# A causal convolution and a three-way maxout layer: one product moved out of the maximum, another order of the stages, a band built by a skewed DMA

## The chip, the cores and the metric

The kernel runs on one core of a Trainium2 chip. The metric is device time in microseconds (us), the median over several executions. All executions reported here are fast ones: granted clock of TensorE (the share of its full clock that the profile records) between 0.987 and 1.0 over the whole span, and times of one kernel within about 0.5% of each other. In the profile, PE is TensorE, PEld its weight loads, DVE VectorE, ACT ScalarE, POOL GpSimd, SP SyncE; a trailing q (SPq, ACTq) is the queue of that engine, from which DMAs are issued. L238 is a line of the kernel's source; line numbers differ between the kernels. PSUM is the memory into which TensorE's products are written in these kernels; ACT and DVE copy or combine them from there. The chain is the work that ended last, followed back step by step to what released it.

## The reference, cut to what matters

```
# x: 8 x 4160 x 192 fp32; weight: 8 heads x 7 taps; w1, w2, w3: 192 x 768; w_out: 768 x 192
w = softmax(weight)                                   # 7 taps for each head of 24 channels
y[s] = sum_k w[head, k] * x[s - 6 + k]                # zeros ahead of each batch's first row
h = maximum(maximum(y @ w1, y @ w2), y @ w3)          # 33280 tokens x 768
out = h @ w_out                                       # 33280 x 192, fp32
```

The 33280 tokens are handled as 65 blocks of 512: 64 whole ones, and one made of the last 64 rows of each of the 8 batches (the "ragged" block).

## The kernel before

For each block, TensorE does the convolution as 40 small matmuls against a banded matrix of the taps (two PSUM tiles G1, G2, 32 rows per head), and ACT copies the result to fp16 (xctA, xctB). The first layer runs per slice of 128 hidden columns, six slices in all: three products of two 512-column matmuls each, one ACT copy and two DVE maxima. The second layer (`emit_st2`) runs for the block before, as 4 x 6 matmuls of 192 columns, all of them between the convolution and the first layer.

```
def emit_st2(t, out_sb):
    for s in range(ceil(N / P)):
        pso = psu.tile([P, NBLK], FP32, tag="ps")
        for j in range(NJ):                                   # NJ = 6
            nc.tensor.matmul(pso[0:ms, 0:D], lhsT=hT[:, j, P * s : P * s + ms], rhs=wo[:, j, :],
                             start=(j == 0), stop=(j == NJ - 1))
        nc.scalar.copy(out=out_sb[0:ms, s, :], in_=pso[0:ms, 0:D])

for t in range(NB):                                           # NB = 65
    emit_xdma(t + 3)
    emit_conv(t, G1, G2)
    if prev is not None:
        emit_st2(tp, out_sb_p)                                # second layer of the block before
    nc.scalar.copy(out=xctA[:, 0:N], in_=G1[:, 0:N])
    nc.scalar.copy(out=xctB[:, 0:N], in_=G2[:, 0:N])
    # ... store of the block before ...
    for j in range(NJ):
        for i in range(3):                                    # w1, w2, w3
            nc.tensor.matmul(psw[i][:, 0:N], lhsT=wg[i][0][:, jj], rhs=xctA[:, 0:N], start=True, stop=False)
            nc.tensor.matmul(psw[i][:, 0:N], lhsT=wg[i][1][:, jj], rhs=xctB[:, 0:N], start=False, stop=True)
        nc.scalar.copy(out=t1[:, 0:N], in_=psw[0][:, 0:N])
        nc.vector.tensor_max(out=t12[:, 0:N], in0=t1[:, 0:N], in1=psw[1][:, 0:N])
        nc.vector.tensor_max(out=hT_t[t][:, j, 0:N], in0=t12[:, 0:N], in1=psw[2][:, 0:N])
        if j == 0:
            emit_xcast(t + 3)                                 # x to fp16, on ACT
```

At the start, DVE builds the band of the convolution from masks and taps (56 instructions), and ACT casts the weights.

The softmax here doesn't subtract the row's maximum and nothing guards it: scores larger than these inputs give would overflow.

Of the kernel before, what the change touches and what calls it, by code (L numbers as in the profile page):

```python
# [7 lines left out]

FP32 = mybir.dt.float32  # L10
FP16 = mybir.dt.float16
INT32 = mybir.dt.int32
AXX = mybir.AxisListType.X
ALU = mybir.AluOpType
# [9 lines left out]
NBLK = 512  # L24


@with_exitstack
def kernel(
# [9 lines left out]
):  # L38
    nc = tc.nc

# [5 lines left out]

    blocks = []
# [4 lines left out]
    segs = []  # L52
    off = 0
    for b in range(B):
        s = nfull * NBLK
        while s < SEQ:
            n = min(SEQ - s, NBLK - off)
            segs.append((b, s, n, off))
            off += n
            s += n  # L60
            if off == NBLK:
                blocks.append(segs)
                segs = []
                off = 0
# [5 lines left out]
    def conv_chunks(blk):  # L70
        res = []
        q = 0
        for (b, S, N, off) in blk:
            qq = 0
            while CHK * qq < N:
                o_lo = CHK * qq
                o_hi = min(o_lo + CHK, N)
                row_lo = max(0, S + o_lo - PAD)
                rlen = min(P, SEQ - row_lo)
                cc_lo = o_lo - (row_lo - S)  # L80
                res.append((q, b, row_lo, rlen, off + o_lo, off + o_hi, cc_lo))
                q += 1
                qq += 1
        return res

    NQMAX = max(len(conv_chunks(blk)) for blk in blocks)

    const = ctx.enter_context(tc.tile_pool(name="const", bufs=1))
    wpool = ctx.enter_context(tc.tile_pool(name="wpool", bufs=1))
    xfp = ctx.enter_context(tc.tile_pool(name="xfp", bufs=4))  # L90
    x16p = ctx.enter_context(tc.tile_pool(name="x16p", bufs=4))
    xctp = ctx.enter_context(tc.tile_pool(name="xctp", bufs=2))
    tmpp = ctx.enter_context(tc.tile_pool(name="tmpp", bufs=2))
    htp = ctx.enter_context(tc.tile_pool(name="htp", bufs=2))
    outp = ctx.enter_context(tc.tile_pool(name="outp", bufs=2))

    psg = ctx.enter_context(tc.tile_pool(name="psg", bufs=2, space=bass.MemoryType.PSUM))
    psu = ctx.enter_context(tc.tile_pool(name="psu", bufs=6, space=bass.MemoryType.PSUM))

    wraw = const.tile([P, NHEAD, KW], FP32)  # L100
    nc.sync.dma_start(
        out=wraw[:],
        in_=bass.AP(tensor=weight.tensor, offset=0, ap=[[0, P], [KW, NHEAD], [1, KW]]),
    )
    idx = const.tile([P, BAND_W], INT32)
    nc.gpsimd.iota(out=idx[:], pattern=[[1, BAND_W]], base=0, channel_multiplier=-1)

    x16_t = {}

    def emit_xdma(t):  # L110
        if not (0 <= t < NB):
            return
        chunks = conv_chunks(blocks[t])
        xf32 = xfp.tile([P, NQMAX, D], FP32, tag="xf32", name=f"xf32_{t}")
        x16 = x16p.tile([P, NQMAX, D], FP16, tag="x16", name=f"x16_{t}")
        x16_t[t] = (xf32, x16, [])
        i = 0
        n = len(chunks)
        while i < n:
            jx = i  # L120
            while (
                jx + 1 < n
                and chunks[jx][3] == P
                and chunks[jx + 1][3] == P
                and chunks[jx + 1][1] == chunks[jx][1]
                and chunks[jx + 1][2] - chunks[jx][2] == CHK
            ):
                jx += 1
            (q0, b0, row_lo0, rlen0, _, _, _) = chunks[i]
            cnt = jx - i + 1  # L130
            if cnt > 1:
                src = bass.AP(
                    tensor=x.tensor,
                    offset=(b0 * SEQ + row_lo0) * D,
                    ap=[[D, P], [CHK * D, cnt], [1, D]],
                )
                nc.sync.dma_start(out=xf32[:, i : jx + 1, :], in_=src)
                x16_t[t][2].append((slice(0, P), slice(i, jx + 1)))
            else:
                nc.sync.dma_start(  # L140
                    out=xf32[0:rlen0, q0, :], in_=x[b0, row_lo0 : row_lo0 + rlen0, :]
                )
                x16_t[t][2].append((slice(0, rlen0), slice(q0, q0 + 1)))
            i = jx + 1

    def emit_xcast(t):
        if not (0 <= t < NB):
            return
        (xf32, x16, parts) = x16_t[t]
        for (ps, qs) in parts:  # L150
            nc.scalar.copy(out=x16[ps, qs, :], in_=xf32[ps, qs, :])  # L151

    for u in range(min(3, NB)):
        emit_xdma(u)
        emit_xcast(u)

    wexp = const.tile([P, NHEAD, KW], FP32)
    nc.scalar.activation(out=wexp[:], in_=wraw[:], func=AF.Exp)  # L158
    wsum = const.tile([P, NHEAD], FP32)
    nc.vector.reduce_sum(out=wsum[:], in_=wexp[:], axis=AXX)  # L160
    wrec = const.tile([P, NHEAD], FP32)
    nc.vector.reciprocal(out=wrec[:], in_=wsum[:])
    wnrm = const.tile([P, NHEAD, KW], FP32)
    for h in range(NHEAD):
        nc.vector.tensor_scalar_mul(
            out=wnrm[:, h, :], in0=wexp[:, h, :], scalar1=wrec[:, h : h + 1]
        )
    masks = const.tile([P, KW, BAND_W], FP32)
    for a in range(KW):
        nc.vector.tensor_scalar(  # L170
            out=masks[:, a, :],
            in0=idx[:],
            scalar1=float(a),
            scalar2=None,
            op0=ALU.is_equal,
        )
    bacc = [
        const.tile([P, BAND_W], FP32, tag=f"bacc{h}", name=f"bacc{h}")
        for h in range(NHEAD)
    ]  # L180
    band = const.tile([P, NHEAD, BAND_W], FP16)
    for k in range(KW):
        a = KW - 1 - k
        for h in range(NHEAD):
            if k == 0:
                nc.vector.tensor_scalar_mul(  # L186
                    out=bacc[h][:], in0=masks[:, a, :], scalar1=wnrm[:, h, 0:1]
                )
            else:
                nc.vector.scalar_tensor_tensor(  # L190
                    out=bacc[h][:],
                    in0=masks[:, a, :],
                    scalar=wnrm[:, h, k : k + 1],
                    in1=bacc[h][:],
                    op0=ALU.mult,
                    op1=ALU.add,
                )
            if k == KW - 1:
                nc.scalar.copy(out=band[:, h, :], in_=bacc[h][:])  # L199

    def slot_ranges(half):
        if half == 0:
            return [(32 * g, GRP * g, GRP) for g in range(4)]
        return [(32 * g, 96 + GRP * g, GRP) for g in range(3)] + [(104, 168, GRP)]

    wg = []
    for i, wsrc in enumerate((moe_w1, moe_w2, moe_w3)):
        halves = []
        for half in range(2):
            stage = wpool.tile([P, DFF], FP32, tag=f"wstage{i}{half}")  # L210
            nc.vector.memset(stage[:], 0.0)  # L211
            for (s0, c0, cnt) in slot_ranges(half):
                nc.sync.dma_start(  # L213
                    out=stage[s0 : s0 + cnt, :], in_=wsrc[c0 : c0 + cnt, :]
                )
            wt = wpool.tile([P, DFF], FP16, tag=f"w{i}{half}")
            nc.scalar.copy(out=wt[:], in_=stage[:])  # L217
            halves.append(wt)
        wg.append(halves)

    wo_stage = wpool.tile([P, NJ, D], FP32)
    nc.sync.dma_start(out=wo_stage[:], in_=moe_w_out.rearrange("(j p) c -> p j c", p=P))
    wo = wpool.tile([P, NJ, D], FP16)
    nc.scalar.copy(out=wo[:], in_=wo_stage[:])

    out_2d = out

    hT_t = {}

    def emit_conv(t, G1, G2):  # L230
        (_, x16, _) = x16_t[t]
        for (q, b, row_lo, rlen, out_lo, out_hi, cc_lo) in conv_chunks(blocks[t]):
            ncols = out_hi - out_lo
            for h in range(NHEAD):
                g = h % 4
                gt = G1 if h < 4 else G2
                cb = GRP * h if h < NHEAD - 1 else GRP * h - 8
                nc.tensor.matmul(  # L238
                    gt[32 * g : 32 * g + 32, out_lo:out_hi],
                    lhsT=x16[0:rlen, q, cb : cb + 32],  # L240
                    rhs=band[0:rlen, h, cc_lo : cc_lo + ncols],
                    start=True,
                    stop=True,
                    tile_position=(0, 32 * g),
                )

    def emit_st2(t, out_sb):
        N = blkN[t]
        hT = hT_t[t]
        for s in range(ceil(N / P)):  # L250
            ms = min(P, N - P * s)
            pso = psu.tile([P, NBLK], FP32, tag="ps", name=f"pso_{t}_{s}")
            for j in range(NJ):
                nc.tensor.matmul(  # L254
                    pso[0:ms, 0:D],
                    lhsT=hT[:, j, P * s : P * s + ms],
                    rhs=wo[:, j, :],
                    start=(j == 0),
                    stop=(j == NJ - 1),
                )  # L260
# [20 lines left out]
    for t in range(NB):  # L281
# [17 lines left out]
        for j in range(NJ):  # L299
# [27 lines left out]
            if j == 0:  # L327
                emit_xcast(t + 3)
# [38 lines left out]
```

## Time and profile before

| kernel before | value | where from |
|---|---|---|
| median time | 772.04 us (771.39 to 773.94, four runs) | times |
| profiled span, granted clock | 770.3 us, 0.997 | profile |
| busy: TensorE, DVE, ACT | 90%, 68%, 56% | page, engine totals |
| one block of 512 tokens | 11.31 us (mean over 60 blocks) | timeline |
| 512-column, 192-column matmul, start to start | 0.216, 0.083 us | timeline |
| stall ahead of the seventh second-layer matmul | 0.78 us, or 0.35 more in some blocks | timeline |

To read it: the page's busy share of TensorE counts matmuls that overlap, so it does not say how much of a block is work. Only the distances in the timeline do. The shares of the chain by line show whose time counts towards the end:

```profile
PE psw L306 27%; PE psw L313 27%; PE pso L254 14%; DVE t L323 11%; DVE hT L324 7%; PE G L238 1%; DVE bacc L190 1%; DMA wo_stage<-in_moe_w_out_dram 1%; DVE stage L211 1%; ACT wt L217 0%; DVEq L324 0%; ACT t L322 0%; DVE bacc L186 0%; SPq L213 0%; ACT outsb L261 0%
```

The three products are 54% of it (L306, L313), the second layer 14%, and the two maxima on DVE (L323, L324) another 18%: the last maximum of a block is what the second layer then waits for.

### The profile page before, as it was taken

To read this page: it belongs to the slowest core of one execution; us is meant where nothing else is said; L and a number is where in the kernel's file an instruction comes from. 1 tells how busy PE (TensorE), PEld (TensorE's weight loads), DVE (VectorE), ACT (ScalarE), POOL (GpSimd) and SP (SyncE) were. 2 spreads that over 40 slices of the span, in tenths; PEclk is the share of its full clock that TensorE was granted. 3 is DMA by queue.
4 is the path that set the end of the run, shared out by engine and by line. 5 is a ranking of instruction groups with operands and counts; after the bars stand their busy time and mean duration, and the time that the engine had idled before them with its cause. 6 is when DMAs were issued, how large, how long until landed. Compare 5 with 4: busy or idle time off the path is not lost.

```text
span 770.3 us, 16387 instructions
## 1 busy us (share of the span) xinstructions
PE 696.2 (90%) x6524; PEld 386.6 (50%) x6524; DVE 527.1 (68%) x859; ACT 429.1 (56%) x885; POOL 0.4 (0%) x5
## 2 busy tenths in 40 slices
PE   0799999999999999999999999999999999999996
PEld 0355555555545554555555555555455545555543
DVE  9476766676676677667667666766766766676674
ACT  3666555556555555555555555555555555556552
POOL 0000000000000000000000000000000000000000
PEclk9999999999999999999999999999999999999998
DMA  6342223133133223313322322331332233111101
GB/s 183 121 143 54 86 91 89 52 93 93 52 88 93 68 73 91 93 49 93 93 52 88 94 76 63 94 93 50 91 92 60 81 93 88 48 43 42 34 31 42
DMA packets 78829, 60.69 MB, mean 79 GB/s; under 512 B 2880, under 2 KB 78176, under 8 KB 78752
## 3 DMA queue, kind: packets, MB, share of 16 engines
q1 hardware_dynamic: 78752, 59.64, 26.3%
q8 instruction: 51, 0.84, 0.5%
q14 instruction: 26, 0.21, 0.1%
HBM read 34.07 MB, written 25.56 MB: 77 GB/s over the span
## 4 chain that ended last, share of the span: by engine, by line
PE 68%; DVE 19%; issue 9%; ACT 1%; DMA 1%; DVEq 0%; SPq 0%; ACTq 0%
PE psw L306 27%; PE psw L313 27%; PE pso L254 14%; DVE t L323 11%; DVE hT L324 7%; PE G L238 1%; DVE bacc L190 1%; DMA wo_stage<-in_moe_w_out_dram 1%; DVE stage L211 1%; ACT wt L217 0%; DVEq L324 0%; ACT t L322 0%; DVE bacc L186 0%; SPq L213 0%; ACT outsb L261 0%
## 5 line engine op out<-in xcount | busy, mean ns | idle before, releaser
L306 PE MATMUL psw<-xctA,wt 128*128 128x512 f16 x1170 | 443.8, 380 | 0.8 <-ACT xctA L292 0.3
L313 PE MATMUL psw<-xctB,wt 128*128 128x512 f16 x1170 | 443.7, 380 | 0.5 <-ACT wt L217 0.4
L323 DVE TENSOR_TENSOR t<-t,psw 128x512 f32<-128x512 f32 x390 | 265.2, 681 | 187.3 <-ACT t L322 180.5
L322 ACT COPY t<-psw 128x512 f32<-128x512 f32 x390 | 228.5, 586 | 230.5 <-PE psw L313 220.8
L324 DVE TENSOR_TENSOR hT<-t,psw 128x512 f16<-128x512 f32 x390 | 267.3, 687 | 46.2 <-PE psw L313 8.3
L254 PE MATMUL pso<-wo,hT 128*128 128x192 f16 x1560 | 151.8, 247 | 42.8 <-DVE hT L324 42.6
L313 PEld LDWEIGHTS <-wt 128*128 128x128 f16 x1170 | 114.4, 98 | 132.7 <-issue 1.9
L306 PEld LDWEIGHTS <-wt 128*128 128x128 f16 x1170 | 114.4, 98 | 130.8 <-issue 0.8
L254 PEld LDWEIGHTS <-hT 128*128 128x128 f16 x1560 | 122.3, 98 | 60.6 <-DVE hT L324 57.4
L261 ACT COPY outsb<-pso 128x192 f32<-128x192 f32 x260 | 71.7, 327 | 35.1 <-PE pso L254 34.9
L151 ACT CAST x<-xf 128x960 f16<-128x960 f32 (+3 forms) x88 | 69.2, 792 | 2.8 <-DMA xf<-in_x_dram 2.8
L292 ACT CAST xctA<-G 128x512 f16<-128x512 f32 x65 | 38.0, 585 | 54.4 <-PE G L238 54.4
L238 PE MATMUL G<-band,x 128*32 128x122 f16 (+3 forms) x2624 | 45.7, 212 | 22.7 <-ACT band L199 21.8
L238 PEld LDWEIGHTS <-x 128*32 128x32 f16 (+2 forms) x2624 | 37.6, 98 | 52.0 <-issue 46.9
L293 ACT CAST xctB<-G 128x512 f16<-128x512 f32 x65 | 38.5, 592 | 0.0
L190 DVE SCALAR_TENSOR_TENSOR bacc<-masks,wnrm,bacc 128x134 f32<-128x134 f32 x48 | 13.0, 347 | 0.0
L199 ACT CAST band<-bacc 128x134 f16<-128x134 f32 x8 | 2.0, 300 | 7.5 <-DVE bacc L190 7.5
L217 ACT CAST wt<-stage 128x768 f16<-128x768 f32 x6 | 5.0, 834 | 1.2 <-DVE bacc L190 0.8
L211 DVE MEMSET stage<- 128x768 f32 x6 | 4.2, 698 | 1.5 <-PEq L351 1.0
L186 DVE TENSOR_SCALAR bacc<-masks,wnrm 128x134 f32<-128x134 f32 x8 | 1.7, 284 | 0.0
L158 ACT ACT_TABLE_LOAD x1 | 1.3, 1283 | 0.7 <-PEq L351 0.7
L158 ACT ACTIVATE wexp<-wraw 128x56 f32<-128x56 f32 x1 | 0.2, 249 | 2.2 <-DMA wraw<-in_weight_dram 2.2
(10 smaller groups left out, 4.3 us busy)
## 6 DMA issues: line engine op xcount, KB each, us to landing
out_dram<-outsb SPq DMA_DIRECT2D x64, 384.0 KB
xf<-in_x_dram SPq DMA_DIRECT2D x48, 480.0 KB
xf<-in_x_dram SPq DMA_DIRECT2D x16, 384.0 KB
stage<-in_moe_w_dram SPq DMA_DIRECT2D x24, 72.0 KB
xf<-in_x_dram SPq DMA_DIRECT2D x8, 96.0 KB
wo_stage<-in_moe_w_out_dram SPq DMA_DIRECT2D x1, 576.0 KB
xf<-in_x_dram SPq DMA_DIRECT2D x8, 70.5 KB
xf<-in_x_dram SPq DMA_DIRECT2D x8, 52.5 KB
```

Of the source, the lines that this page charges most:

```text
L151: nc.scalar.copy(out=x16[ps, qs, :], in_=xf32[ps, qs, :])
L190: nc.vector.scalar_tensor_tensor(out=bacc[h][:], in0=masks[:, a, :], scalar=wnrm[:, h, k : k + 1], in1=bacc[h][:], op0=ALU.mult, op1=ALU.add,)
L238: nc.tensor.matmul(gt[32 * g : 32 * g + 32, out_lo:out_hi], lhsT=x16[0:rlen, q, cb : cb + 32], rhs=band[0:rlen, h, cc_lo : cc_lo + ncols], ...
L254: nc.tensor.matmul(pso[0:ms, 0:D], lhsT=hT[:, j, P * s : P * s + ms], rhs=wo[:, j, :], start=(j == 0), stop=(j == NJ - 1),)
L261: nc.scalar.copy(out=out_sb[0:ms, s, :], in_=pso[0:ms, 0:D])
L292: nc.scalar.copy(out=xctA[:, 0:N], in_=G1[:, 0:N])
L293: nc.scalar.copy(out=xctB[:, 0:N], in_=G2[:, 0:N])
L306: nc.tensor.matmul(psw[i][:, 0:N], lhsT=wg[i][0][:, jj], rhs=xctA[:, 0:N], start=True, stop=False,)
L313: nc.tensor.matmul(psw[i][:, 0:N], lhsT=wg[i][1][:, jj], rhs=xctB[:, 0:N], start=False, stop=True,)
L322: nc.scalar.copy(out=t1[:, 0:N], in_=psw[0][:, 0:N])
L323: nc.vector.tensor_max(out=t12[:, 0:N], in0=t1[:, 0:N], in1=psw[1][:, 0:N])
L324: nc.vector.tensor_max(out=hT_t[t][:, j, 0:N], in0=t12[:, 0:N], in1=psw[2][:, 0:N])
```

## The change

The intent is less work for TensorE and DVE. With a = y@w1, b = y@w2, c = y@w3, max(a, b, c) = c + max(a-c, b-c, 0). The maximum needs only the two products y@(w1-w3) and y@(w2-w3), and c@w_out is y@m with m = w3@w_out, a 192 x 192 matrix made once on the chip. ACT's copy becomes a relu, DVE has one maximum per slice. The other parts: the cast of x moves from ACT to GpSimd; the copies of the output go from ACT to DVE; second-layer quarters are interleaved with first-layer slices in an order fixed by hand; the band comes from DRAM by a DMA whose rows are skewed (each row is read from one position earlier than the row above it).

```
-            nc.scalar.copy(out=x16[ps, qs, :], in_=xf32[ps, qs, :])
+            nc.gpsimd.tensor_copy(out=x16[0:rl, q0:q1, :], in_=xf[0:rl, q0:q1, :])
...
-    for k in range(KW):                     # band: 56 DVE instructions on masks
-        ... scalar_tensor_tensor(out=bacc[h][:], in0=masks[:, a, :], scalar=wnrm[:, h, k : k + 1], ...)
+    for k in range(KW):
+        nc.vector.tensor_mul(out=R[:, P - 1 + KW - 1 - k, :], in0=wexp[:, k, :], in1=wrec[:])
+    nc.scalar.dma_start(out=Rd[:], in_=R[:].rearrange("p u h -> p (u h)"))        # to DRAM
+    nc.scalar.dma_start(out=bandc[:].rearrange("p c h -> p (c h)"),               # skewed, back
+        in_=bass.AP(tensor=Rd[:].tensor, offset=Rd[:].offset + (P - 1) * NHEAD,
+                    ap=[[(RLEN - 1) * NHEAD, P], [1, BAND_W * NHEAD]]))
+    nc.vector.tensor_copy(out=band[:].rearrange("p h c -> p c h"), in_=bandc[:])
...
+    for i, wa in enumerate((w1s, w2s)):
+        for half in range(2):
+            nc.vector.tensor_sub(out=d16[:, half, :], in0=wa[:, half, :], in1=w3s[:, half, :])
+    def make_m():     # 12 fp32 transposes of w3, then 12 fp32 matmuls with w_out, into m16 (fp16)
...
+    def l1(t, j):
+        for i in range(2):
+            for half in range(2):
+                nc.tensor.matmul(ps[i][:, 0:N], lhsT=wd[i][:, half, P * j:P * (j + 1)],
+                                 rhs=y[:, half, 0:N], start=(half == 0), stop=(half == 1))
+        nc.scalar.activation(out=r[:, 0:N], in_=ps[0][:, 0:N], func=AF.Relu)
+        nc.vector.tensor_max(out=hs[t][:, j, 0:N], in0=r[:, 0:N], in1=ps[1][:, 0:N])
+    def st2(t, s):
+        for half in range(2):
+            nc.tensor.matmul(ps[:, s % 2, :], lhsT=y[:, half, sl], rhs=m16[:, half, :],
+                             start=(half == 0), stop=False)
+        for j in range(NJ):
+            nc.tensor.matmul(ps[:, s % 2, :], lhsT=hT[:, j, sl], rhs=wo[:, j, :],
+                             start=False, stop=(j == NJ - 1))
+        if s % 2 == 1:
+            nc.vector.tensor_copy(out=outs[t][0][:, s - 1:s + 1, :], in_=ps[:])
...
+    conv(0)
+    for t in range(NB + 1):
+        if t < NB:
+            load_x(t + 3); cast_x(t + 2)                      # shortened
+            l1(t, 0)
+            conv(t + 1)
+            l1(t, 1)
+            for j in range(2, NJ):
+                st2(t - 1, j - 2)
+                l1(t, j)
+            if t == 0:
+                make_m()
+        else:
+            for s in range(4):
+                st2(t - 1, s)
+        store(t - 1)
```

## The prediction

> **What bounds the kernel now.** I read the engine totals, then the costliest groups, then TensorE's timeline over one block, then the chain of waits, and the start and the end last. One core runs, its granted clock is 0.997, and its span of 770.3 us stands for the timed 771.44.
>
> ```profile
> PE 696.2 (90%) x6524; PEld 386.6 (50%) x6524; DVE 527.1 (68%) x859; ACT 429.1 (56%) x885; POOL 0.4 (0%) x5
> ...
> L306 PE MATMUL psw<-xctA,wt 128*128 128x512 f16 x1170 | 443.8, 380 | 0.8 <-ACT xctA L292 0.3
> L313 PE MATMUL psw<-xctB,wt 128*128 128x512 f16 x1170 | 443.7, 380 | 0.5 <-ACT wt L217 0.4
> L323 DVE TENSOR_TENSOR t<-t,psw 128x512 f32<-128x512 f32 x390 | 265.2, 681 | 187.3 <-ACT t L322 180.5
> L322 ACT COPY t<-psw 128x512 f32<-128x512 f32 x390 | 228.5, 586 | 230.5 <-PE psw L313 220.8
> L324 DVE TENSOR_TENSOR hT<-t,psw 128x512 f16<-128x512 f32 x390 | 267.3, 687 | 46.2 <-PE psw L313 8.3
> L254 PE MATMUL pso<-wo,hT 128*128 128x192 f16 x1560 | 151.8, 247 | 42.8 <-DVE hT L324 42.6
> ```
> TensorE is 90% busy, but its matmuls overlap (380 ns is the length of one, not the distance to the next), so the distances have to be read from the timeline. DVE runs 6 x 2 max instructions per block of 512 tokens; there are 65 blocks. In TensorE's timeline one block ends like this (start, length, and idle before):
>
> ```profile
> 398.17 0.38 PE L306 MATMUL psw<-xctA,wt 128*128 128x512 f16 x1
> 398.38 0.38 PE L313 MATMUL psw<-xctB,wt 128*128 128x512 f16 x1
> 398.69 0.65 PE L238 MATMUL G<-band,x 128*32 128x122 f16 x40
> 399.28 0.67 PE L254 MATMUL pso<-wo,hT 128*128 128x192 f16 x6
> 400.56 1.66 PE L254 MATMUL pso<-wo,hT 128*128 128x192 f16 x18 [0.61 <-DVE hT L324]
> 402.05 0.38 PE L306 MATMUL psw<-xctA,wt 128*128 128x512 f16 x1
> ```
> The reader sees: 512-column matmuls start every 0.216 us; 18 matmuls of the second layer take 402.05 - 400.56 = 1.49 us, 0.083 us each; the 40 conv matmuls take 0.59 us up to the next start, with 0.09 us lost before them (0.31 where 0.22 is normal). Six of the second layer should take 0.50 us but the seventh starts 1.28 us later: a stall of 0.78 us, until DVE has written the last hT. A block is thus 36 x 0.216 + 0.68 + 24 x 0.083 + 0.78 = 11.23 us, which is the distance seen from 391.04 to 402.27. Some blocks stall 0.35 us longer: the second-layer groups at 72.63 and at 750.93 in the chain are 60 blocks apart, 11.31 us each. **So TensorE's stream sets the time, and the tail of DVE's work adds 7% once per block**: DVE's pair of max takes 1.39 us per slice of 128 hidden columns, TensorE's six matmuls 1.30 us. The chain of waits shows the same mix:
>
> ```profile
> PE 68%; DVE 19%; issue 9%; ACT 1%; DMA 1%; DVEq 0%; SPq 0%; ACTq 0%
> ```
> Start: the first conv runs at 21.1 us, the first layer-one matmul at 24.3. The last second-layer matmul starts at 762.6; 65 x 11.31 = 735 before its end, so the start is worth 28 us in effect. After it, copies and eight stores of 48 KB, issued in 5.02 us by one queue, take until 770.3.
>
> [...]
>
> **The change part by part.**
>
> *First layer.* Two products (w1-w3, w2-w3) in place of three: 12 matmuls of 512 fewer per block, 12 x 0.216 = 2.59 us less on TensorE. It lies wholly on the path.
>
> *Second layer.* c is added as y@(w3@w_out): two more 192-column matmuls per 128 tokens, 8 x 0.083 = 0.66 us more, on the path.
>
> *Evacuation.* DVE has one max per slice in place of two (it reads an fp16 relu out of SBUF and one PSUM tile), and takes over the output copies[...]. ACT has 6 relus and 2 y copies at 0.586 = 4.7 us. Both are far below TensorE's block, so the bound stays on TensorE.
>
> *Order.* The order of instructions shows first layer 0, conv of the next block, first layer 1, then second-layer quarters of the block before, alternating with first-layer slices. A hidden slice needs about 0.42 us (matmul to ACT, as 391.04 to 391.46) + 0.58 + 0.05 + 0.69 after its second matmul, some 2.0 us after its first. The last slice of a block is read by the second layer only 0.86 + 0.86 + 0.67 + 0.86 = 3.25 us after its start. A PSUM pair is used again two slices later, 2 x (0.86 + 0.66) = 3.0 us in most places, and 2.4 us at the closest, where its second bank is wanted 2.8 us after the start. I expect the 0.78 us stall to go, entirely.
>
> Block: 24 x 0.216 + 32 x 0.083 + 0.68 = 5.18 + 2.65 + 0.68 = **8.51 us**, against 11.31. For 65 blocks with one conv ahead of the loop: 65 x 7.83 + 64 x 0.68 = 552.5 us.
>
> *x cast on GpSimd.* ACT loses 0.99 us per block. [...] it has 8.5 us and runs a block ahead. Hidden.
>
> *Band.* The 56 DVE instructions of 14.7 us go. In their place is a chain of waits: weight load, exp and seven small products (ready at some 6.2 us, as 5.87 + 0.145 x 7 in the trace before), a 534 KB store to DRAM, a skewed load of 274 KB, a copy on DVE. An estimate of 4.5 to 5.5 us for the store and 4 for the load, beside 1.2 MB of other loads at the 180 to 330 GB/s that the DMA view shows in the first 20 us: band at about 16.5 us.
>
> *Weights.* This is the part of the start that I distrust. In DVE's order the memset of w1's tile stands behind the band copy, and w1 and w2 come in 16 DMAs from ACT's queue, behind the band load. At 0.55 us an issue (24 in 13.16 us before) they end at 18 + 16 x 0.55 = 27, land 2 us later, and one subtraction (0.96 us) is left. First layer one flows from about **29.5 us**, so the start gains nothing on its 28.
>
> *make_m.* After the first layer of block 0, TensorE does 12 fp32 transposes and 12 fp32 matmuls of 192 columns, with DVE copies between. [...] 7 to 16 us; I take **12**, all of it on the path.
>
> *End.* 0.6 us waiting for the last hT; then eight stores from one queue as before, of which the first starts 1.3 us before TensorE ends: 7 us.
>
> Sum: 29.5 + 552.5 + 12 + 0.6 + 7 = 601.6; +1.1 us of time over span as before; +2 for handovers that I can't see: **605 us**, 0.78 of before.
>
> **The rivals.** (a) *TensorE stalls anew*: ACT takes the two y copies ahead of a relu, delaying that slice by some 0.7 us, and slack at the tightest bank is 0.8 us. If 0.3 us per block is lost, the time is 625. For it: the DVE stall of before was of this kind. Against: the sums above leave room. (b) *GpSimd or DVE becomes the bound*: a cast above 8.5 us would do it; 10 us per block means 690. [...] (c) *Start and make_m eat more*: weight DMAs that wait for each other's semaphores and slow fp32 matmuls could add 15 us: 620. (d) *Transfers*: 0.86 MB per 8.5 us is 104 GB/s, while the trace shows over 320 in its first slices; loads run three blocks ahead. Hidden. (e) *Clock*: a denser TensorE might be throttled; before, with 90% busy, it was not.
>
> **Range and chances.** A block is sure to 0.1 us if there is no stall (6 us), start to 4, make_m to 5; surprises are mostly upward. 8 in 10: 588 to 632. Faster by over 2% needs below 756, for which a block would have to cost 10.8 us: 0.97. Within 2%: 0.02. Slower: 0.01.
>
> **What would show it.** Right: second-layer groups 8.5 us apart in TensorE's timeline, idle before them near zero, distances of 0.216 and 0.083 kept; DVE about 60% busy, ACT 55%; GpSimd's cast under 2.5 us; first layer-one matmul between 27 and 32 us; m's matmuls taking 7 to 16 us from first transpose to the next layer-one matmul. Wrong: idle before layer-one matmuls released by ACT or DVE in each block (rival a), waits of conv for the x cast (b), a granted clock below 0.98 (e), or a block of other length without waits, which would mean that the distances don't carry over when the two layers alternate.

The sum came to 29.5 + 552.5 + 12 + 0.6 + 7 = 601.6 us, with 1.1 and 2 added 605; the 12 us for making m (and its range of 7 to 16) was the author's estimate: the trace of the kernel before has no fp32 matmul. Cut as well are the sum of DVE's work per block (of which that trace shows the maxima, 6 x 0.687 = 4.1 us, but no copy of 384 elements), the estimate for GpSimd's cast (that trace has none) and the argument against rival (b); that DVE stays far below TensorE and that the cast is hidden was expected, not shown, at that point.

## The result, and the profile after

The changed kernel takes 599.52 us (599.0 to 600.87, four runs), against 772.04 in the same rounds: a ratio of 0.7763, 95% interval 0.7749 to 0.7777. Here and below a ratio is the mean time of one kernel's fast runs over that of the other's of the same rounds, so not quite the ratio of the medians quoted. The profiled span is 597.4 us, the granted clock 0.997, the result correct.

The page of the changed kernel, engine totals, chain by engine and by line, and the costliest groups (busy us and mean ns of one, then idle before them):

```profile
PE 562.2 (94%) x6300; PEld 361.1 (60%) x6300; DVE 342.9 (57%) x542; ACT 299.2 (50%) x523; POOL 72.0 (12%) x95
...
PE 94%; DMA 3%; DVE 1%; ACT 1%; ACTq 0%; issue 0%; SPq 0%
...
L238 PE MATMUL l<-y,wd 128*128 128x512 f16 x1560 | 392.4, 381 | 9.0 <-ACT y L228 9.0
L242 DVE TENSOR_TENSOR h<-r,l 128x512 f16<-128x512 f16 x390 | 268.2, 688 | 224.8 <-ACT r L241 220.4
L241 ACT ACTIVATE r<-l 128x512 f16<-128x512 f32 x390 | 234.1, 600 | 235.2 <-PE l L238 235.2
...
L256 PE MATMUL pso<-wo,h 128*128 128x192 f16 x1560 | 171.4, 246 | 0.4 <-DVE h L242 0.4
...
L127 POOL CAST x<-xf 128x960 f16<-128x960 f32 (+3 forms) x88 | 70.0, 800 | 487.3 <-DMA xf<-in_x_dram 358.0
...
L259 DVE COPY o<-pso 128x384 f32<-128x384 f32 x130 | 71.6, 551 | 1.8 <-PE pso L256 1.8
```

TensorE's share of the chain went from 68% to 94%, and DVE's from 19% to 1%. The second layer waited 42.6 us for DVE before; it now waits 0.4 us, in one place (after the last slice of the last block). The first layer's 9.0 us of idle time is also one place, the start. DVE and ACT wait 220 and 235 us for their inputs, which costs nothing: they are no longer the engines that others wait for. In TensorE's timeline one block reads (start, length):

```profile
391.34 1.89 PE L238 MATMUL l<-y,wd 128*128 128x512 f16 x8
393.16 0.65 PE L221 MATMUL G<-band,x 128*32 128x122 f16 x40
393.75 1.04 PE L238 MATMUL l<-y,wd 128*128 128x512 f16 x4
394.62 0.33 PE L253 MATMUL pso<-m,y 128*128 128x192 f16 x2
394.79 0.66 PE L256 MATMUL pso<-wo,h 128*128 128x192 f16 x6
...
399.85 1.89 PE L238 MATMUL l<-y,wd 128*128 128x512 f16 x8
```

The block is 399.85 - 391.34 = 8.51 us, with no "idle before" on any line. Four first-layer matmuls take 394.62 - 393.75 = 0.87 us, 0.217 each; two of y@m take 0.17 us and six of the second layer 0.49 us, 0.082 to 0.085 each. The distances of the kernel before carry over to the new order.

The start, from the trace's timeline over all engines:

```profile
10.30 0.35 ACTq L149 DMA_DIRECT2D bandc<-Rd  x1
15.77 2.53 DVE L154 COPY band<-bandc 128x1072 f16<-128x1072 f16 x1 [9.51 <-DMA bandc<-Rd]
...
19.90 6.73 ACTq L170 DMA_DIRECT2D ws<-in_moe_w_dram  x16
...
28.36 1.93 PE L238 MATMUL l<-y,wd 128*128 128x512 f16 x4 [8.96 <-ACT y L228]
...
28.60 0.96 DVE L186 TENSOR_TENSOR wd<-ws,ws 128x768 f16<-128x768 f32 x1 [0.60 <-DMA ws<-in_moe_w_dram]
...
31.20 6.06 PE L238 MATMUL l<-y,wd 128*128 128x512 f16 x20
...
37.10 1.04 PE L198 MATMUL pt<-ident,ws 128*128 128x128 f32 x8
...
39.44 4.17 PE L204 MATMUL pm<-wos,w3t 128*128 128x192 f32 x24
...
43.44 1.03 PE L238 MATMUL l<-y,wd 128*128 128x512 f16 x4
```

The reader sees three things. (Against the kernel before, the convolution starts earlier, at 18.35 us in place of 21.12, but the first layer later, at 28.36 in place of 24.29.) The weights are issued from ACT's queue until 26.6 us and the last difference is ready at 29.56. The first four matmuls take 1.93 us where the steady block has 1.03, so TensorE starts at half of its speed (0.43 us apart, until about 34.5 us). Making m takes from 37.10 to 43.44, 6.3 us, and nothing else of the path runs beside it.

### The profile page after: what moved, and what is told of

Same layout as the page of the kernel before. It is cut to its first block, busy times and chain, and to the rows that moved or that the text cites. A ratio compares the mean times of both kernels' runs of the same rounds, so it can differ in the third digit from the quotient of the medians.

```text
span 597.4 us, 15039 instructions
## 1 busy us (share of the span) xinstructions
PE 562.2 (94%) x6300; PEld 361.1 (60%) x6300; DVE 342.9 (57%) x542; ACT 299.2 (50%) x523; POOL 72.0 (12%) x95
## 4 chain that ended last, share of the span: by engine, by line
PE 94%; DMA 3%; DVE 1%; ACT 1%; ACTq 0%; issue 0%; SPq 0%
PE l L238 58%; PE pso L256 22%; PE pso L253 7%; PE G L221 6%; DMA xf<-in_x_dram 1%; PE pm L204 1%; DMA ws<-in_moe_w_dram 1%; DMA wk<-in_weight_dram 1%; DMA Rd<-R 1%; ACTq L170 0%; DVE h L242 0%; DVE ws L167 0%; ACT r L241 0%; ACT wo L189 0%; SPq L116 0%
## 5 line engine op out<-in xcount | busy, mean ns | idle before, releaser
L238 PE MATMUL l<-y,wd 128*128 128x512 f16 x1560 | 392.4, 381 | 9.0 <-ACT y L228 9.0
L242 DVE TENSOR_TENSOR h<-r,l 128x512 f16<-128x512 f16 x390 | 268.2, 688 | 224.8 <-ACT r L241 220.4
L241 ACT ACTIVATE r<-l 128x512 f16<-128x512 f32 x390 | 234.1, 600 | 235.2 <-PE l L238 235.2
L238 PEld LDWEIGHTS <-wd 128*128 128x128 f16 x1560 | 143.8, 98 | 121.2 <-DVE wd L186 9.6
L256 PE MATMUL pso<-wo,h 128*128 128x192 f16 x1560 | 171.4, 246 | 0.4 <-DVE h L242 0.4
L256 PEld LDWEIGHTS <-h 128*128 128x128 f16 x1560 | 132.7, 98 | 0.6 <-DVE h L242 0.6
L127 POOL CAST x<-xf 128x960 f16<-128x960 f32 (+3 forms) x88 | 70.0, 800 | 487.3 <-DMA xf<-in_x_dram 358.0
L253 PE MATMUL pso<-m,y 128*128 128x192 f16 x520 | 85.4, 246 | 0.0
L228 ACT CAST y<-G 128x512 f16<-128x512 f32 x130 | 69.8, 589 | 28.0 <-PE G L221 28.0
L259 DVE COPY o<-pso 128x384 f32<-128x384 f32 x130 | 71.6, 551 | 1.8 <-PE pso L256 1.8
```

Of the source, the lines that this page charges most:

```text
L127: nc.gpsimd.tensor_copy(out=x16[0:rl, q0:q1, :], in_=xf[0:rl, q0:q1, :])
L228: nc.scalar.copy(out=y[:, i, 0:N], in_=G[i][:, 0:N])
L238: nc.tensor.matmul(ps[i][:, 0:N], lhsT=wd[i][:, half, P * j:P * (j + 1)], rhs=y[:, half, 0:N], start=(half == 0), stop=(half == 1))
L241: nc.scalar.activation(out=r[:, 0:N], in_=ps[0][:, 0:N], func=AF.Relu)
L242: nc.vector.tensor_max(out=hs[t][:, j, 0:N], in0=r[:, 0:N], in1=ps[1][:, 0:N])
L253: nc.tensor.matmul(ps[:, s % 2, :], lhsT=y[:, half, sl], rhs=m16[:, half, :], start=(half == 0), stop=False)
```

## The experiments

My theory was that the gain is the smaller work of TensorE's stream, that the stall disappears by itself, and that the new order and the cast on GpSimd matter little. The main rival was that the hand-made order carries a good part of the gain. Ten kernels were run, each with three or more rounds. All are the changed kernel with the edit shown (e6 builds on e5, e8 on e6 and e7, e9 on e8), and all were correct except the one that is wrong. Two parts of the change were not tested alone: the band built by a DMA, and the output copies on DVE.

### e1: the new arithmetic in the old order

```
-            l1(t, 0)
-            conv(t + 1)
-            l1(t, 1)
-            for j in range(2, NJ):
-                st2(t - 1, j - 2)
-                l1(t, j)
+            conv(t)
+        for s in range(4):
+            st2(t - 1, s)
+        store(t - 1)
+        if t < NB:
+            for j in range(NJ): l1(t, j)          # and make_m() once, shortened
```

> The changed kernel in the old order: per block the conv, then the whole second layer of the block before, then six first-layer slices; nothing else differs. Theory 'less work' (one max per slice in place of two leaves DVE nothing to finish when the second layer wants the last h): last h lands some 2.03 us after its slice starts, and is wanted 0.86 + 0.67 + 7 x 0.083 = 2.1 us after; the stall is at most 0.1 us, a block 8.5 to 8.6 us, the time 598 to 607 us. Rival 'order' (the interleaving hid the last h): the old stall of 0.78 us per block is back, 65 x 0.78 = 51 us more, about 650 us.

Measured: 600.13 us (599.04 to 600.47), ratio 0.7764 [0.7752, 0.7776]; the span is 597.3 us. TensorE's timeline of e1:

```profile
391.39 0.65 PE L221 MATMUL G<-band,x 128*32 128x122 f16 x40
...
394.62 5.34 PE L238 MATMUL l<-y,wd 128*128 128x512 f16 x24
399.89 0.65 PE L221 MATMUL G<-band,x 128*32 128x122 f16 x40
```

The block is 399.89 - 391.39 = 8.50 us, without any idle time ahead of the second layer. The order gives nothing once the work is less: DVE has one maximum of 0.69 us per slice, which is shorter than the four matmuls of a slice (0.86 us), so it finishes close behind TensorE; by the count in the expectation, some 0.1 us ahead of being wanted. The rival falls.

### e2: the new order with three products

```
-    for i, wa in enumerate((w1s, w2s)):
+    for i, wa in enumerate((w1s, w2s, w3s)):                 # copied, not subtracted
-        nc.scalar.activation(out=r[:, 0:N], in_=ps[0][:, 0:N], func=AF.Relu)
-        nc.vector.tensor_max(out=hs[t][:, j, 0:N], in0=r[:, 0:N], in1=ps[1][:, 0:N])
+        nc.scalar.copy(out=r[:, 0:N], in_=ps[0][:, 0:N])
+        nc.vector.tensor_max(out=r2[:, 0:N], in0=r[:, 0:N], in1=ps[1][:, 0:N])
+        nc.vector.tensor_max(out=hs[t][:, j, 0:N], in0=r2[:, 0:N], in1=ps[2][:, 0:N])
# also: no y@m and no m; output copies back on ACT; one ring of four PSUM banks for the products
```

> The changed kernel with the three products of before (copy of the first on ACT, two max per slice on DVE, no y@m, no m), in the new interleaved order; output copies on ACT so that DVE has no more than before; the first-layer PSUM ring is 4 banks. TensorE's stream is then 36 x 0.216 + 24 x 0.083 + 0.68 = 10.45 us per block. Theory 'order can hide it too': no stall, 65 blocks of 10.45 and a start of 29, end of 7: about 716 us. Rival 'less work': DVE's lag (1.39 us of max per slice) still meets the second layer, blocks near 11.3, about 765 to 772 us. In both, the products are worth at least 716 - 599.5 = 116 us.

Measured: 718.21 us (717.78 to 719.11), ratio 0.9296 [0.9282, 0.931]. TensorE's timeline of e2:

```profile
391.93 2.75 PE L238 MATMUL l<-y,wd 128*128 128x512 f16 x12
394.61 0.65 PE L221 MATMUL G<-band,x 128*32 128x122 f16 x40
...
402.36 1.89 PE L238 MATMUL l<-y,wd 128*128 128x512 f16 x8
```

The block is 402.36 - 391.93 = 10.43 us, against 11.31, and again without idle time. So with three products the stall goes too, in the new order. With e1 this makes a table of four (medians in us):

| | old order | new order |
|---|---|---|
| three products, two maxima | 772.0 | 718.2 |
| two products, one maximum, y@m | 600.1 | 599.5 |

Order is worth 54 us without the new arithmetic, arithmetic 172 us without the new order, both together 172.5: the two parts remove the same stall, and their gains do not add.

The upper left kernel is the one before, though: its cast of x runs on ACT, its output copies are shorter and twice as many, its two layers share one ring of PSUM banks, and its start is another (first layer-one matmul at 24.3 us, in e2 at 27.8). No run changes the order alone. The trace of the kernel before speaks against its cast and copies as the cause of the stall: in the block from 390.83 us the first product is complete at 391.42, ACT starts on it at 391.46, and DVE then runs its twelve maxima without a wait from 392.08 to 400.50, just before the stall ends at 400.56.

In the new order, where neither kernel stalls, the products are worth 118.7 us. Per block that is 12 x 0.216 less 8 x 0.083, 1.93 us, or 125 us for 65 blocks, less the 6.3 us of making m.

### e3: the cast of x back on ACT

```
-            nc.gpsimd.tensor_copy(out=x16[0:rl, q0:q1, :], in_=xf[0:rl, q0:q1, :])
+            nc.scalar.copy(out=x16[0:rl, q0:q1, :], in_=xf[0:rl, q0:q1, :])
```

> The changed kernel with the x cast back on ACT (0.99 us per block, at the head of a block's first relu). Theory 'TensorE alone binds': the delayed relu stays within the 0.8 us to 1.2 us of slack of its PSUM bank, time 599 to 602 us. Rival 'the cast had to leave ACT': the first slice of each block stalls TensorE by 0.2 us or more, 613 us or above.

Measured: 601.07 us (600.97 to 601.68), ratio 0.7781 [0.7768, 0.7794]. The 1.6 us more come from the start, as the view of waits of e3 shows (total us, times, longest):

```profile
PE G L221 <- ACT x L127: 27.7, 2, 27.4
```

ACT issues the weights' DMAs, and its cast of the first x stands behind them, so the first convolution starts at 27.4 us and the first layer at 30.52 in place of 28.36. The other such wait is 0.3 us; the blocks do not stall. In the steady part the engine of the cast does not matter.

### e4: without y@m (wrong on purpose)

```
-        for half in range(2):
-            nc.tensor.matmul(ps[:, s % 2, :], lhsT=y[:, half, sl], rhs=m16[:, half, :],
-                             start=(half == 0), stop=False)
```

> Wrong result on purpose: the changed kernel without the y@m matmuls (8 of 192 columns per block; m is still made). Theory 'every matmul is on the path': 65 x 8 x 0.083 = 43 us less, 556 us, second-layer quarters 0.50 us. Rival 'the evacuation chain is as long as the stream': ACT and DVE waits take their place, less than 25 us gained, 575 us or more.

Measured: 555.73 us (555.01 to 557.15), ratio 0.7194 [0.7182, 0.7207]; the output is wrong, as intended. The span fell by 597.4 - 553.2 = 44.2 us for 65 x 8 matmuls, 0.085 us each. The removed matmuls cost their full distance: TensorE's stream is the bound, and within the 0.68 us that a block lost, nothing else took its place.

### e5: the weights' loads ahead of the band's

```
+    nc.vector.memset(w1s[:], 0.0)          # memsets first
+    nc.vector.memset(w2s[:], 0.0)
+    load_w(w1s, moe_w1, nc.scalar)         # w1 ahead of the bandc load in ACT's queue
     nc.scalar.dma_start(out=bandc[:]...)
+    load_w(w2s, moe_w2, nc.scalar)
     # the two subtractions of w1 ahead of the band copy on DVE
```

> Only the order of the start is changed: DVE clears the weight tiles before it waits for the band, and ACT's queue gives w1's DMAs before the band load and w2's right after it; the same instructions otherwise. Theory 'the band chain held the weights back': w2 lands near 19 us instead of 27, first layer-one matmul near 21 us instead of 28.4, time about 592 us. Rival 'the start is bound by bytes' [...]: the DMAs only take longer, gain under 2 us, 597.5 us or more.

(The ground given for the rival was not shown, and is cut.)

Measured: 597.42 us (596.55 to 598.12), ratio 0.7733 [0.772, 0.7747]; the first layer starts at 27.80 us, only 0.56 us earlier. A miss: the gain of 2.1 us is about what the rival allowed. The windows of 18 to 22 us (busy time of PE, PEld, DVE, ACT, POOL, then granted clock, DMA share and GB/s), first of the changed kernel, then of e5:

```profile
18.00:22.00 4.00, 1.05 (x40) 0.95 (x39) 2.97 (x3) 0.00 (x0) 2.99 (x3) 1.00 0.44 133
```

```profile
18.00:22.00 4.00, 0.00 (x0) 0.00 (x0) 0.91 (x1) 0.00 (x0) 1.27 (x2) 1.00 1.10 307
```

In the changed kernel the DMA engines are half idle there, waiting for weights to be issued. e5 fills that gap, but its shares from 2 us on, in windows of 4 us, are 0.72, 0.84, 0.90, 1.08, 1.10: the transfers themselves seem to be the limit then, and the band's load is the one that comes later. Part of that is the edit's own doing, as w1's loads now stand ahead of it in ACT's queue: it was issued at 16.08 us in place of 10.30, and the first convolution came at 25.78 in place of 18.35. So e5 alone does not separate the bytes from the queue. e9 (below) does so better: there the band's load is issued at 15.49 us, also behind w1, but DVE finds it landed at 18.79, while in e5 it could start the copy only at 23.20.

### e6: e5, and m made before the first convolution

```
-            if t == 0:
-                make_m()
+    make_m()                               # right after its definition, ahead of the subtractions
```

> The start of the run before, and m made while TensorE waits for the band, not after block 0. Theory 'make_m lies wholly on the path': 6.3 us (37.1 to 43.4 in the changed kernel) come off, 586 us; if the slow first matmuls (0.43 us apart from 28.4 to 34.5) are due to a TensorE that was idle before, up to 2.5 us more, 583 us. Rival 'm then delays conv': DVE copies of m hold back the band copy, 590 us or more.

Measured: 590.43 us (590.22 to 593.2), ratio 0.7655 [0.7635, 0.7674], 7.0 us less than e5 on the same chip (6.3 by the means, of which one run of 593.2 is part), where 6.3 were expected if making m lies wholly on the path. The step is right; the level is above the 586 because e5 had missed its own. The number alone would also fit the rival, that m delays the convolution (590 or more), but the trace does not: the first convolution starts at 24.42 us, in e5 at 25.78.

e6 also shows something odd. TensorE's first layer at half speed, in windows of the changed kernel and of e6 (the number after the five busy times is the granted clock):

```profile
28.00:34.50 6.50, 6.13 (x52) 2.44 (x52) 2.34 (x4) 3.49 (x7) 0.99 (x1) 1.00 0.01 3
```

```profile
26.00:30.00 4.00, 3.01 (x45) 1.39 (x45) 1.65 (x2) 2.09 (x5) 0.82 (x1) 0.50 0.05 15
```

Both have the first four 512-column matmuls in 1.93 us. Of the two, only e6 shows a granted clock of 0.50; the changed kernel shows 1.00. The distances have to be trusted here, not the view's clock. The packed trace says why: the changed kernel's first clock event is the step to full speed, at 34.42 us, where the slow distances end, and the view counts the time before the first event as 1.00.

### e7: the ragged block moved to the middle

```
+    blocks.insert(len(blocks) // 2, blocks.pop())
```

> The changed kernel with the block of eight 64-row pieces moved from the end to the middle. Theory 'the eight issues of the last store (5.02 us) set the end': TensorE's end to the last landing falls from 6.9 to 3.5 us, time about 596 us. Rival 'they overlap with the landing of the first': under 1 us, 599 us; or the pieces stall the middle of the run: above 600 us.

Measured: 596.72 us (596.34 to 596.98), ratio 0.7727 [0.7716, 0.7739], 2.8 us less where 3.5 were expected. The last stores, in the timeline of the changed kernel:

```profile
589.89 5.02 SPq L273 DMA_DIRECT2D out_dram<-o  x8
590.63 0.56 DVE L259 COPY o<-pso 128x384 f32<-128x384 f32 x1 [0.76 <-PE pso L256]
```

Eight issues of one queue run until 594.9 and the last one lands by 597.4, though the last copy was done at 591.2. In e7 the last block is a whole one with a single store; the time from TensorE's end to the span's end is 4.4 us in place of 6.8.

### e8 and e9: the three together

e8 joins e6 and e7, puts the band's copy on ACT, and stores the last block in two halves:

```
-    nc.vector.tensor_copy(out=band[:].rearrange("p h c -> p c h"), in_=bandc[:])
+    nc.scalar.copy(out=band[:].rearrange("p h c -> p c h"), in_=bandc[:])
```

> All three together, with the band copy on ACT and the last block stored in two halves. If the gains add: 599.5 - 7 - 6.3 - 3.5 - 0.5, about 582 us; 580 if TensorE is also warm. If they don't add (the band then sets the first conv, near 18 us): 588 us. This should be faster than both kernels.

Measured: 592.8 us (591.79 to 593.09), ratio 0.7675 [0.7663, 0.7686]. A miss by 11 us. The timeline of e8 has the reason:

```profile
25.98 4.93 ACT L205 COPY band<-bandc 128x1072 f16<-128x1072 f16 x1 [20.91 <-DMA ws<-in_moe_w_dram]
```

The copy reads in one order and writes in another. On ACT it took 4.93 us where DVE took 2.53, and it could start only when ACT had issued the last DMA of w2, at 25.9 us. The first convolution came at 30.96 us. So e9 puts it back on DVE, moves w2's loads to SP's queue, ahead of the loads of the next blocks' x, and copies m late, on ACT:

```
-    load_w(w2s, moe_w2, nc.scalar)
+    load_w(w2s, moe_w2, nc.sync)           # after w_out, ahead of load_x(1), load_x(2)
+    nc.vector.tensor_copy(out=band[:].rearrange("p h c -> p c h"), in_=bandc[:])
+    for half in range(2):
+        nc.scalar.copy(out=m16[:, half, :], in_=pms[half][:])
```

> The second start version (m made while waiting) with the ragged block in the middle and the last store in two halves, and with w2 ahead of x1 to x4 on the sync queue, so that the DMA engines, 0.7 to 1.1 busy until 22 us in the runs before, bring first what block 0 needs. If the start is bound by those transfers: first layer-one matmul at 21 to 23 us instead of 27.0, and 2.8 us from the tail: 580 to 583 us. If it is bound by DMAs that wait for each other's completion: it stays near 27 us, 587 us.

Measured: 582.94 us (582.28 to 583.12), ratio 0.7552 [0.7541, 0.7564]. This beats both kernels: 16.6 us below the changed one. Its timeline has the first layer 5.6 us earlier:

```profile
22.72 1.93 PE L242 MATMUL l<-y,wd 128*128 128x512 f16 x4 [0.68 <-ACT y L232]
```

With 6.3 us for m off the path and 3.2 us less after TensorE's end (3.6 in place of 6.8), these three are 15.1 of the 16.4 us by which the span fell. e9 changed w2's queue, its place and the copies of m at once, so what each is worth is not shown.

### e10: dummy matmuls ahead of the first layer

After the idle stretch TensorE's matmuls are 0.43 us apart, for 6 us. To test whether idleness is the cause, 34 matmuls on a constant tile fill the wait between the first convolution and the first layer:

```
     conv(0)
+    warm(34, "warm")                       # 34 x 512 columns into a PSUM tile that nobody reads
```

> The changed kernel with 34 idle 512-column matmuls on TensorE between the first conv and the first layer-one matmul (their result is not read; the output is right). Theory 'an idle TensorE starts at half speed' (layer-one matmuls 0.43 us apart from 28.4 to 34.5 us, though the page shows a clock of 1.00 there): they end near 28 us, the matmuls after them are 0.216 us apart at once, 2 to 2.5 us less: 597 us. Rival 'the slow start comes from waits on weights or evacuation': distances stay 0.43, time 599.5 or above.

Measured: 597.98 us (597.12 to 598.8), ratio 0.7745 [0.7732, 0.7758], within the expected range but only 1.5 us below the changed kernel, and 0.4 us in span. The timeline of e10:

```profile
21.33 8.40 PE L284 MATMUL warm<-dm 128*128 128x512 f16 x34 [0.25 <-POOL dm L279]
...
30.06 1.48 PE L238 MATMUL l<-y,wd 128*128 128x512 f16 x4 [0.33 <-ACT y L228]
...
32.05 4.79 PE L238 MATMUL l<-y,wd 128*128 128x512 f16 x20
```

The first layer of block 0 with the convolution now takes from 30.06 to 36.67, 6.6 us, where the changed kernel needs 28.36 to 37.10, 8.7. The dummies themselves start slow, 0.43 us apart until 23.2 us, though they read only a constant tile and nobody reads their result. So in these traces the slow distances go with the idle stretch ahead of them: 20.0 us before the convolution and the dummies of e10, 8.96 us before the first layer of the changed kernel. After 8.4 us of dummies and a gap of 0.33 us, the first layer of e10 isn't slow: its 20 matmuls from 32.05 us on take 4.79, 0.23 us apart. It takes less than 9 us of idleness: in e9 the first layer starts slow (1.93 us for four) after gaps of only 1.75 and 0.68 us, with one convolution at full speed (0.65 us) between them. The slow stretch lasted 3.2 us in e10 (20.02 to 23.2), 3.6 in e9 (22.72 to 26.3), and 6.1 from the first layer on in the changed kernel (28.36 to 34.42); what sets its length is not shown. The 2.1 us were nearly given back because the band and with it the first layer came 1.7 us later in this profiled run. Why the band came later is not settled; the dummies themselves begin only after it. The profiled execution is the slowest of e10's four; the fastest has a span of 595.3 us, 2.1 below the 597.4.

## Why the prediction was right

The predicted time was 605 us and the measured one 599.5, inside the range. The mechanism was right. Of the sizes, making m and the unseen handovers were together 7.7 us too high, the start and the time over span 2.5 us too low; that these partly cancel is luck. By its own steps, in us:

| term of the sum | predicted | measured | how read |
|---|---|---|---|
| start, as if the first layer flowed from there | 29.5 | 31.2 | 37.10 less 24 x 0.216 less 0.68 |
| 65 blocks and 64 convolutions | 552.5 | 552.5 | 8.51 from block to block, as predicted |
| making m | 12 | 6.3 | 37.10 to 43.44 |
| wait for the last h | 0.6 | 0.4 | page, second layer's idle time |
| after TensorE | 7 | 6.8 | last matmul ends at 590.6, span 597.4 |
| time over span | 1.1 | 1.9 | profiled run 599.25 less 597.4 |
| handovers that I couldn't see | 2 | 0 | no idle time in the blocks |

- **The block** was right to the hundredth: 24 x 0.216 + 32 x 0.083 + 0.68. e4 confirms the price of a second-layer matmul, and e1 and e2 show that the stall is gone with either part; the step from e2 to the changed kernel (118.7 us, 119 by the distances) fits that of a first-layer one. The prediction said "I expect the 0.78 us stall to go, entirely", and named slack in the new order as the reason. That is one of two sufficient reasons: e1 shows that a single maximum per slice is enough without the order.
- **Making m** was mis-sized, by 5.7 us: "7 to 16 us; I take 12". The working of the estimate is cut; the trace has these parts. Its weight loads run beside the matmuls: 3.9 us of loads against 4.17 us of matmuls, both from 39.44. Twelve products take (43.44 - 39.44) / 12 = 0.33 us each (two records each in the trace), four times the 0.083 us of an fp16 matmul of 192 columns, and a transpose 0.11 to 0.13 us (eight in 1.04 us, four in 0.66, the last one's length of 0.27 among them). So the sign that m's matmuls take 7 to 16 us did not come. That all of it lies on the path was right: e6 gained 6 to 7 us by moving it.
- **The start** was mis-sized in the other direction, and for a reason that isn't in the prediction. The transfers went as written: issue of the weights ended at 26.6 us (27 predicted), the last subtraction started 2.0 us later, took 0.96 us, and was ready at 29.56. The band came at 18.3 us, not 16.5, as its copy took 2.5 us, but it was not what the first layer waited for: that was ACT's copy of the convolution (27.73 us), behind the issues of the weights and the cast of w_out on ACT. What I left out is that TensorE, idle for 9 us, starts at half speed (0.43 us apart in place of 0.216). The first layer and one convolution took 8.7 us in place of 5.9, so an earlier first matmul (28.36) was worth less than it looks.
- **The rivals.** No new stall (a), GpSimd at 12% and DVE at 57% (b), no throttled steady clock (d, e: 0.997, and no wait of TensorE on a transfer in the blocks); (c), more at the start, was true by 1.7 us and outweighed by m. One sum of (b) was wrong: blocks of 10 us would give about 702 us by the prediction's own terms, not 690. GpSimd's cast of 128x960 took 0.99 us, and the output copy on DVE 0.551 us, so that DVE's work in a block is 6 x 0.688 + 2 x 0.551 = 5.2 us, below TensorE's 8.51.

## What to carry to other kernels

When one engine's stream is dense, count its instructions times their start-to-start distance from the timeline: this gave a changed block to the hundredth of a microsecond, and the work removed from that stream paid in full. Two remedies for the same stall don't add; measure each without the other (here 54 and 172 us, together 172.5). After the steady part is settled, look at the ends: the order of loads at the start, one-time work on the bound engine, and a last block that stores in many small pieces were worth another 16.6 us.
